# First transform with 64 points and two products a bank, U of the first block through scratch: an FNet and H3 kernel on one core of Trainium2

## The chip, the cores and the metric

The kernel runs on one core of one Trainium2 chip. The metric is the device time of one execution in microseconds (us). TensorE (PE) multiplies matrices, with its weight loads listed as PEld; VectorE (DVE), ScalarE (ACT) and GpSimd (POOL) work element by element; SyncE (SP) issues most transfers, ScalarE and GpSimd the others. All engines run their own lists of instructions in order and wait for each other by semaphores.

## The reference

x has 2048 rows (S) of 576 (D). Four layers are applied, A, B, A, B:

```python
x = x + _A_ref(layernorm(x), dft_seq_re, dft_seq_im, dft_hid_re, dft_hid_im)
x = x + _B_ref(layernorm(x), k, v, shift_k, ssm_k, ssm_D)
# and the same two once more

# A: a = x @ hid_re.T, b = x @ hid_im.T;  y = seq_re @ a - seq_im @ b
# B: k_shift = causal convolution of k with 4 taps;  kv = k_shift * v
#    y = irfft(rfft(kv, 4096) * rfft(ssm_k, 4096))[:2048] + kv * ssm_D;  y = q * y   (q is layernorm(x))
```

In B the part before the product with q depends on the inputs k, v, shift_k, ssm_k and ssm_D alone. It is the same for both B layers and is computed once.

## The kernel before

All large products are made on fp32 split into a rounded high part and a remainder (`split`: ScalarE writes the high part, VectorE the remainder), so that a product of two such numbers takes three TensorE instructions: high by high, high by low, low by high.

**The first A layer** runs over 128 steps (tb, g, k): four blocks of 512 output rows, two halves (real and imaginary DFT matrix, `c_mat`) and 16 pieces of the sum over the sequence. A step loads one 128 x 512 piece of c two steps ahead, splits it, and issues 14 products of 512 columns into four banks (s0 to s3) and one for the remaining 64 columns (rm). After 16 steps `evac_u` and `evac_r` split the banks into the chunks of U, nine of 128 x 1024 words in one region (`um`), which the next block overwrites. The rows X[j] of the normalized x are made in the first 16 steps (`get_x0`, `normed`, `to_x`).

**The hidden products** (`hidden`) multiply a finished block's U by W, the hidden DFT matrix: eight pieces a block, each 27 products of 288 columns into a bank (bk). They wait in `pending` and are issued by `finish` between the steps: odd steps of the next block, and what is left ahead of the last step of a half (`yield n, None`), because that step overwrites U. W is loaded and split by `load_w` from step `W_FROM` on, in the region where the branch kept k and its convolution, and is saved to scratch from step `W_SAVE` on.

**The branch** (`branch`) computes the part of B that depends on inputs alone, as a fast Fourier transform in stages, interleaved with the layer's steps. The first transform stage (`f1_split`, `f1_products`) has 32 items: 16 rows j from two sources, ssm_k and k_shift * v. For an item it multiplies by a 128-point matrix `fc`: two halves of 288 columns and two outputs, real and imaginary, three products a bank. ScalarE copies the bank out (`so`) and stores it to scratch (t). The convolution of k runs beside it on VectorE (`convolve`). From step `MID_FROM` on the middle stage loads t back: 64 mid groups of nine products and 32 inverse groups of six, spread by a count of work done (`spent`, `passed`, `total`) until step `I2_END`.

Where in the steps the first transform stands is set by these lines: up to step 16 `F1_16` sets the pace, then it is even until `F1_END` (42).

```python
at16 = 4 + 2 * F1_16
want = int(4 + F1_16 * at / 8 if at <= 16 else at16 + (68 - at16) * (at - 16) / (F1_END - 16))
```

**The second A layer** runs its first block in 32 such steps and the three others by Strassen's scheme; its 32 hidden pieces end the kernel. The last block's pieces of the first layer are issued between its first steps. The change does not touch it otherwise.

The order in which an engine's instructions stand is set by the program's order, by `behind` and `issue_after`, and by the framework's scheduling. Transfers through SP's queue are issued in order, one behind the other.

## Time and profile before

| | |
|---|---|
| median of 3 runs | 1202.72 us (1202.7 to 1205.96) |
| the profiled execution | 1201.11 us, span 1199.3 us |
| first product, last product of TensorE | 6.56 us, about 1191.6 us |
| busy: PE, DVE, ACT, POOL | 98%, 70%, 56%, 6% of the span |
| granted TensorE clock | 0.998 |
| moved by DMA | 261.96 MB, mean 218 GB/s |
| read from and written to HBM | 194.09 MB, 66.65 MB |

The page gives busy times for the whole span, 40 slices of it, groups of instructions and the chain of work that ended last. Its groups go by line, operation and tiles: bk<-f1r are the products of the first transform, bk<-mid those of the middle stage, bk<-w,u the hidden products of the first A layer, s and rm those of the steps. A group's mean is the length of one instruction; TensorE's instructions overlap, so their spacing is read from the timeline.

### The profile page before, as it was taken

What the parts mean: (1) busy time and instruction counts of PE and PEld (TensorE: products, weight loads), DVE (VectorE), ACT (ScalarE), POOL (GpSimd) and SP (SyncE); (2) the same over time, 40 slices, a digit from 0 to 9 for tenths busy, and PEclk for the clock granted to TensorE, in tenths of its full rate; (3) what the DMA queues carried; (4) which work ended last, traced back from release to release, by engine and by line L of the source; (5) the groups of instructions that cost most, each with busy time, mean ns of one, the idle gap of its engine ahead of it and who ended that gap; (6) DMA issues with size and microseconds to landing.
All of it is one profiled execution on the core that took longest, in us unless ns stands there. A gap on an engine that the chain in (4) does not pass through costs nothing.

```text
span 1199.3 us, 18263 instructions
## 1 busy us (share of the span) xinstructions
PE 1180.6 (98%) x6320; PEld 1026.0 (86%) x6320; DVE 839.9 (70%) x1498; ACT 665.9 (56%) x1335; POOL 75.5 (6%) x116
## 2 busy tenths in 40 slices
PE   7999999999999999999999999999999999999997
PEld 6888888988888888888988898888888888789997
DVE  7899883679777677675447766875676777774674
ACT  8855665679877768675435666544444435450210
POOL 2210000000000000001101121000000000001111
PEclk9999999999999999999999999999999999999999
DMA  9879898546656766658967686872772677794621
GB/s 340 308 226 318 275 304 256 177 133 182 216 177 199 213 180 207 187 149 249 305 202 236 222 257 213 271 264 71 216 281 74 207 275 269 237 347 142 214 96 40
DMA packets 146111, 261.96 MB, mean 218 GB/s; under 512 B 15841, under 2 KB 44769, under 8 KB 146018
## 3 DMA queue, kind: packets, MB, share of 16 engines
q1 hardware_dynamic: 102674, 205.58, 53.6%
q10 hardware_dynamic: 36432, 42.63, 10.3%
q0 software_dynamic: 6912, 12.59, 4.1%
q8 instruction: 49, 0.80, 0.3%
q14 instruction: 44, 0.36, 0.1%
HBM read 194.09 MB, written 66.65 MB: 217 GB/s over the span
## 4 chain that ended last, share of the span: by engine, by line
PE 84%; DVE 6%; DMA 4%; ACT 3%; issue 2%; POOL 1%; SPq 0%; POOLq 0%; DVEq 0%; ACTq 0%
PE s L74 46%; PE bk L74 33%; PE rm L74 5%; DMA flts<-in_c_mat 2%; ACT flts L486 1%; DVE mats L92 1%; DVE f1f L382 1%; DMA flts<-t 1%; POOL flts L616 1%; DVE mats L189 1%; ACT mid L486 1%; DVE f1f L387 0%; DMA t<-flts 0%; DVE u L92 0%; ACT mats L91 0%
## 5 line engine op out<-in xcount | busy, mean ns | idle before, releaser
L74 PE MATMUL s<-mats 128*128 128x512 f32 x2088 | 531.2, 392 | 0.8 <-DVE flts L613 0.3
L74 PEld LDWEIGHTS s<-mats 128*128 128x128 f32 x2088 | 381.1, 188 | 71.1 <-DVE mats L189 1.1
L92 DVE TENSOR_TENSOR mats<-flts,mats 128x512 fp32r<-128x512 f32 x206 | 140.7, 688 | 58.4 <-ACT mats L91 55.7
L91 ACT ACTIVATE mats<-flts 128x512 fp32r<-128x512 f32 x206 | 128.2, 627 | 85.4 <-PE bk L74 30.9
L74 PE MATMUL bk<-mid 128*128 128x288 f32 x768 | 131.1, 300 | 1.8 <-ACT flts L486 0.8
L74 PEld LDWEIGHTS bk<-mid 128*128 128x128 f32 x768 | 114.3, 188 | 21.2 <-ACT flts L486 8.4
L492 DVE TENSOR_TENSOR mid<-flts,mid 128x576 fp32r<-128x576 f32 (+1 forms) x160 | 101.9, 637 | 34.4 <-ACT mid L486 31.3
L74 PE MATMUL bk<-w,u 128*128 128x288 f32 x864 | 121.0, 296 | 0.7 <-DVE w L232 0.5
L74 PEld LDWEIGHTS bk<-w,u 128*128 128x128 f32 x864 | 117.4, 188 | 4.4 <-ACT flts L486 1.1
L486 ACT ACTIVATE flts<-bk 128x288 f32<-128x288 f32 x160 | 61.9, 404 | 87.4 <-PE bk L74 74.0
L74 PE MATMUL rm<-mats 128*128 128x512 f32 x304 | 94.9, 391 | 0.0
L486 ACT ACTIVATE mid<-flts 128x576 fp32r<-128x576 f32 (+1 forms) x159 | 86.8, 582 | 7.5 <-DMA flts<-t 3.7
L486 ACT ACTIVATE flts<-flts 64x288 f32<-64x288 f32 x192 | 85.0, 443 | 5.7
L432 ACT ACTIVATE flts<-bk 128x288 f32<-128x288 f32 x128 | 49.4, 408 | 47.0 <-PE bk L74 46.4
L74 PEld LDWEIGHTS bk<-f1r 128*128 128x128 f32 x384 | 59.5, 191 | 13.8 <-ACT f1r L91 7.4
L74 PE MATMUL bk<-f1r 128*128 128x288 f32 x384 | 64.5, 300 | 6.7 <-ACT f1r L91 6.7
L74 PE MATMUL bk<-mats 128*128 128x288 f32 (+1 forms) x376 | 67.8, 317 | 0.0
L74 PEld LDWEIGHTS rm<-mats 128*128 128x128 f32 x304 | 57.0, 188 | 12.1 <-DVE flts L264 0.3
L74 PE MATMUL s<-t,mats 128*128 128x512 f32 x264 | 64.9, 389 | 0.0
L278 DVE TENSOR_TENSOR flts<-flts,bk 128x288 f32<-128x288 f32 x48 | 21.7, 453 | 61.1 <-PE bk L74 58.8
L175 POOL TENSOR_TENSOR flts<-flts 128x1 f32<-128x1 f32 x35 | 28.9, 827 | 524.2 <-DVE flts L174 524.2
L74 PE MATMUL bk<-mats,t 128*128 128x288 f32 (+1 forms) x368 | 59.3, 303 | 0.0
(143 smaller groups left out, 1491.8 us busy)
## 6 DMA issues: line engine op xcount, KB each, us to landing
flts<-in_c_mat SPq DMA_DIRECT2D x148, 256.0 KB, 3.6
ph<-in_c_mat SPq DMA_DIRECT2D x54, 512.0 KB, 3.9
t<-flts ACTq DMA_DIRECT2D x64, 288.0 KB, 4.6
flts<-t SPq DMA_DIRECT2D x64, 288.0 KB, 2.9
flts<-in_c_mat SPq DMA_DIRECT2D x30, 512.0 KB, 5.3
vd<-flts ACTq DMA_DIRECT2D x64, 144.0 KB, 2.5
flts<-vd SPq DMA_DIRECT2D x32, 288.0 KB, 4.8
mid<-in_i2c POOLq DMA_DIRECT2D x32, 256.0 KB, 5.6
```

The costliest lines, as they stand in the source:

```text
L74: nc.tensor.matmul(ps, lhsT, rhs, start=first, stop=last, skip_group_check=more)
L91: a = nc.scalar.activation(h, src, AF.Copy).ins
L92: return a, nc.vector.tensor_tensor(l, src, h.bitcast(F32), OP.subtract).ins
L175: pows.append(nc.gpsimd.tensor_tensor(rs, ve, mhalf, OP.pow).ins)
L189: made.append(nc.vector.tensor_tensor(t[:, D + REM:], y[:, :NC * P], h[:, :NC * P], OP.subtract).ins)
L278: added[:] = [nc.vector.tensor_tensor(r[:, cs], r[:, cs], ps[:, :HD], OP.add).ins]
L382: nc.vector.tensor_tensor(out_t[:, n], k, wt[3 - t][:, n], OP.mult)
L432: stored[:] = [nc.scalar.activation(so[:, c, :], ps[:, :HD], AF.Copy).ins]
L486: last_act.append(nc.scalar.activation(*args, **kw).ins)
L492: nc.vector.tensor_tensor(l, src, h.bitcast(F32), OP.subtract)
L616: pows.append(nc.gpsimd.tensor_tensor(rs, sv, mhalf, OP.pow).ins)
```

## The change

The first transform has 64 points: on the host the rows of k, v and ssm_k are put in another order, even rows on partitions 0 to 63 and odd rows on 64 to 127, and the matrices are made for 32 sets of 64 rows. The split now puts the high part of 64 rows and their remainder on top of each other on 128 partitions, so that one product takes both; a bank needs two products, one with the high and one with the low part of the matrix. The stage's pace is `F1_PACE`, which ends at step 55.5. So W, which takes the convolution's place, is loaded from step 55 on. The first block's U is stored to scratch (`us_d`) chunk by chunk from step 33 on, loaded back in steps 72 to 76, and multiplied by W in steps 78 and 79; the second block's pieces come before, from step 64 on. The middle stage begins at step 61, and W is saved from step 80 on, every third step. The number and size of the transfers of t stay; the matrix of the middle stage now has 32 points on its first side.

```diff
-F1_END = 42
-W_FROM = 41
+F1_PACE = (0, 14, 16, 30, 32.5, 46, 48, 55.5), (4, 8.5, 9, 27, 28, 49.5, 50.5, 68)
+F1_END = 56
+W_FROM = 55
-W_SAVE = 60
-MID_LOAD = 44
-MID_FROM = 47
+W_SAVE = 80
+MID_LOAD = 57
+MID_FROM = 61
+SPILL = {33: 8, 36: 0, 39: 1, 42: 2, 45: 3, 51: 4, 54: 5, 57: 6, 60: 7}
+REFILL = {72: (0, 1), 73: (2, 3), 74: (4, 5), 75: (6, 7), 76: (8,)}
+PIECES = (*range(64, 72), 78, *range(97, 111, 2))
@@
-    t_d = [dr.tile([P, J, 2, 2, HD], F32, name=f"t{h}") for h in range(2)]
+    t_d = [dr.tile([P, 2, J, 2, HD], F32, name=f"t{h}") for h in range(2)]
+    us_d = [dr.tile([P, WIDE], F32, name=f"us{ch}") for ch in range(9)]
@@
+    spilled = []
+
+    def spill(ch):
+        load_after(us_d[ch], um[0][:, ch * WIDE:(ch + 1) * WIDE].bitcast(F32))
+
+    def refill(ch):
+        load_after(um[0][:, ch * WIDE:(ch + 1) * WIDE].bitcast(F32), us_d[ch])
+        if ch == 8:
+            pending.extend(spilled)
@@ layer
-                    pending.extend([us, tb, jj, xres, done] for jj in range(TB))
+                    (pending if tb else spilled).extend([us, tb, jj, xres, done] for jj in range(TB))
@@ f1_split
-            parted[:] = split(xf[0], xf[1], r)
+            sides = (xf[0], lo, hi), (xf[1], hi, lo)
+            if (j, src) == todo[0]:
+                h = [nc.scalar.activation(xf[0][lo], r[lo], AF.Copy).ins, nc.vector.tensor_copy(xf[1][hi], r[hi]).ins]
+            else:
+                h = [nc.scalar.activation(t[at], r[at], AF.Copy).ins for t, at, to in sides]
+            with behind(h[1]):
+                parted[:] = h + [nc.vector.tensor_tensor(t[to], r[at], t[at].bitcast(F32), OP.subtract).ins
+                                 for t, at, to in sides]
@@ f1_products
-                for c in range(2):
+                for h in range(2):
                     ps = bank()
-                    mm(ps[:, :HD], fc[:, c, :], xf[0][:, cs], True, False)
-                    mm(ps[:, :HD], fc[:, c, :], xf[1][:, cs], False, False)
-                    mm(ps[:, :HD], fc[:, 2 + c, :], xf[0][:, cs], False, True)
-                    stored[:] = [nc.scalar.activation(so[:, c, :], ps[:, :HD], AF.Copy).ins]
-                nc.scalar.dma_start(t_d[hf][:, j, :, src, :], so)
+                    mm(ps[:, :HD], fc[:, 2 * h, :], xf[h][:, cs], True, False)
+                    mm(ps[:, :HD], fc[:, 2 * h + 1, :], xf[h][:, cs], False, True)
+                    stored[:] = [nc.scalar.activation(so[:, h, :], ps[:, :HD], AF.Copy).ins]
+                nc.scalar.dma_start(t_d[hf][:, :, j, src, :], so)
@@ branch, its loop over the items
+            if n == 1:
+                yield from f1_products(*split_up.pop())
+                split_up.append((j, src, f1_split(j, src), fcs[j]))
+                f1_loads(n + 3)
+                continue
@@ the loop over the steps
-    first_lo = parted[1]
+    first_lo = parted[2]
     next(br)
     next(br)
     with behind(first_lo):
         get_x0(1)
-    next(br)
-    next(br)
+    with behind(*rounded):
+        next(br)
+        next(br)
...
-            at = n if whole else n - 0.5
-            at16 = 4 + 2 * F1_16
-            want = int(4 + F1_16 * at / 8 if at <= 16 else at16 + (68 - at16) * (at - 16) / (F1_END - 16))
+            want = int(np.interp(n if whole else n - 0.5, *F1_PACE))
...
-            if whole is None or whole and n % 2 == 1 and n % (2 * J) < J - 1 and pending:
+            if whole is None or whole and n in PIECES:
                 finish(pending, 1)
...
-        if n >= W_SAVE and n % 2 == 0:
+        if n in SPILL:
+            spill(SPILL[n])
+        for ch in REFILL.get(n, ()):
+            refill(ch)
+        if n >= W_SAVE and n % 3 == 0:
             next(wl, 0)
```

The changes of the host code (the order of the rows and the matrices) are left out.

More of the change, by code (lines that the diff above doesn't have):

```diff
@@ L338, in branch @@
     def branch():
+        lo, hi = slice(0, 64), slice(64, 128)
         f1r = region_b(FR, "f1r")
@@ L362, in load_k @@
                                   bass.AP(tensor=k_pad.tensor, offset=k_pad.offset + 2 * i * D,
-                                          ap=[[J * D, P], [1, 2 * D]]))
+                                          ap=[[(J + 4) * D, P], [1, 2 * D]]))
                 k_loaded[0] += 1
@@ L471, in branch @@
         load_fr(mc, midc)
-        lo, hi = slice(0, 64), slice(64, 128)
         def mid_half(df, o):
@@ L552, in load_feed @@
                 load_after(landed[i], v_d[hf][:, q].rearrange("p c d -> p (c d)") if kind else
-                           t_d[hf][4 * q:4 * q + 4].rearrange("q j c s d -> (q j c) (s d)"))
+                           t_d[hf][4 * q:4 * q + 4].rearrange("x h j s d -> (x h j) (s d)"))
         def load_fc(k):
@@ L1049, in _constants @@
     ang = 2 * np.pi * n / 8192
-    f1 = [_parts(np.cos(ang)), _parts(-np.sin(ang))]
-    f1c = np.stack([f1[0][0], f1[1][0], f1[0][1], f1[1][1]], axis=2)
-    at = ang.transpose(0, 2, 1)
+    h = P // 2
+    n = (32 * p[None, :h, None] + np.arange(2 * J)[:, None, None]) * (4 * q[None, None, :h] + 1) % 8192
+    f1 = np.stack([np.cos(2 * np.pi * n / 8192), -np.sin(2 * np.pi * n / 8192)], axis=3)
+    f1 = np.stack(_parts(f1.reshape(2, J, h, P)), axis=1).transpose(2, 3, 0, 1, 4).reshape(J, h, 4, P)
+    f1c = np.concatenate([f1, f1], axis=1)
+    at = ang.transpose(0, 2, 1)[:, (p % 2) * h + p // 2]
     i2 = [_parts(np.cos(at) / S), _parts(-np.sin(at) / S)]
@@ L1055, in _constants @@
     th = 2 * np.pi * (j[:, None] * r[None, :] % J) / J
-    f2 = np.zeros((4, J, 2, 2, 4, J))
     i1 = np.zeros((2, 4, J, 4, J, 2))
@@ L1059, in _constants @@
     for a in range(4):
-        f2[a, :, 0, 0, a, :] = c
-        f2[a, :, 1, 0, a, :] = s
-        f2[a, :, 0, 1, a, :] = -s
-        f2[a, :, 1, 1, a, :] = c
         i1[0, a, :, a, :, 0] = c.T
@@ L1067, in _constants @@
         i1[1, a, :, a, :, 1] = c.T
+    r = np.arange(2 * J)
+    th = 2 * np.pi * (r[:, None] * (r // J + r % J * 2)[None, :] % 32) / 32
+    f2 = np.zeros((2, 2, 2 * J, 2, 2, 2 * J))
+    c, s = np.cos(th), np.sin(th)
+    for a in range(2):
+        f2[a, 0, :, 0, a, :] = c
+        f2[a, 1, :, 0, a, :] = s
+        f2[a, 0, :, 1, a, :] = -s
+        f2[a, 1, :, 1, a, :] = c
     m = [*_parts(f2.reshape(P, P)), *_parts(i1.reshape(P, P))]
@@ L1080, in perm, with halved @@
         return m.transpose(1, 4, 3, 2, 0)
+    def halved(m):
+        return m.reshape(P // 2, 2, -1).transpose(1, 0, 2).reshape(P, -1, D)
     f1c, i2c, midc = _constants()
+    k = np.pad(a["B_k"][0], ((3, 1), (0, 0)))
     arrays = {
@@ L1087 @@
         "w_im": a["A_dft_hid_im"].T,
-        "k_pad": np.pad(a["B_k"][0], ((3, 1), (0, 0))),
-        "v": a["B_v"].reshape(P, J, D),
+        "k_pad": halved(np.stack([k[J * i:J * i + J + 4] for i in range(P)])),
+        "v": halved(a["B_v"]),
         "shift_k": a["B_shift_k"].T,
-        "ssm_k": a["B_ssm_k"].T.reshape(P, J, D),
+        "ssm_k": halved(a["B_ssm_k"].T),
         "ssm_d": a["B_ssm_D"],
```

## The prediction

> **What bounds the kernel now.** The first view is the page's table of busy times, with the rows of the 40 slices for TensorE (PE) and the DMA engines.
>
> ```profile
> PE 1180.6 (98%) x6320; PEld 1026.0 (86%) x6320; DVE 839.9 (70%) x1498; ACT 665.9 (56%) x1335; POOL 75.5 (6%) x116
> PE   7999999999999999999999999999999999999997
> DMA  9879898546656766658967686872772677794621
> ```
>
> TensorE is busy from the second slice to the last but one. Its busy time overlaps from product to product, so I take spacings instead, from the timeline (start, length, engine, what): one layer step without other work, the end of the kernel, and six first-transform products from the chain of waits.
>
> ```profile
> 628.50 2.88 PE L74 MATMUL s<-mats 128*128 128x512 f32 x12
> 631.68 2.88 PE L74 MATMUL s<-mats 128*128 128x512 f32 x12
> ```
> ```profile
> 1167.52 2.56 PE L74 MATMUL bk<-mats 128*128 128x288 f32 x18
> 1171.11 2.53 PE L74 MATMUL bk<-mats 128*128 128x288 f32 x18
> ```
> ```profile
> 194.18 0.79 PE bk L74 x6
> 194.97 1.37 PE s L74 x6
> ```
>
> A step (14 products of 512 columns) starts every 3.18 us, 0.227 each. Two bank fills (27 products of 288 columns) take 3.59 us, 0.133 each; six among layer products take 0.79, 0.132 each. I use 3.17 for a step (0.2266 a product) and 0.132. By its loops the kernel has 3,440 products of 512 columns and 2,880 of 288, together the page's 6,320: 779.5 + 380.2 = 1159.7 us of a span of 1199.3. Some 40 us are lost; the windows (PE, PEld, DVE, ACT, POOL busy, clock, DMA share, GB/s) show where.
>
> ```profile
> 0.00:20.78 20.78, 14.22 (x60) 11.61 (x61) 15.27 (x48) 15.67 (x26) 5.02 (x13) 1.00 0.97 335
> 20.78:70.26 49.48, 49.04 (x235) 40.78 (x234) 42.98 (x92) 41.55 (x89) 12.85 (x13) 1.00 0.86 297
> 70.26:200.17 129.91, 129.72 (x695) 112.52 (x694) 107.44 (x128) 77.08 (x172) 5.28 (x10) 1.00 0.88 278
> 200.17:618.72 418.55, 415.75 (x2371) 363.93 (x2370) 283.39 (x539) 286.12 (x615) 17.44 (x33) 1.00 0.65 200
> 618.72:1199.30 580.58, 571.83 (x2970) 497.22 (x2968) 390.86 (x693) 245.50 (x436) 34.87 (x48) 1.00 0.63 207
> 107.12:131.22 24.10, 24.10 (x133) 21.10 (x132) 24.06 (x27) 13.56 (x30) 1.58 (x3) 1.00 1.03 340
> 281.54:325.87 44.33, 44.33 (x235) 38.33 (x234) 37.26 (x75) 38.91 (x84) 0.00 (x0) 1.00 0.63 196
> ```
>
> The first five end at the start of steps 3, 16, 43 and 111 and at the end. The order of the program gives the products in each: 3 steps and 19 first-transform products, 12.0 of 20.78 us, 8.8 lost; 13 steps and 50, 47.8 of 49.48, 1.7 lost; 27 steps and 315, 127.2 of 129.91, 2.7 lost; 68 steps and 1,416, 402.5 of 418.55, 16 lost; the rest 11. So a product taken away is worth its spacing, unless another engine becomes late. VectorE (DVE) is the nearest: in 107.12 to 131.22 it is busy 24.06 of 24.10 us, and TensorE loses nothing.
>
> **The change part by part.**
>
> **1. Products, −16.9 us.** A bank of the first transform takes two products in place of three: 32 items with 4 banks each, 256 in place of 384. All have 128 rows, 128 columns and 288 moving columns as before, since the rounded part and the remainder of 64 rows are stacked into 128. 128 x 0.132 = 16.9. The Trainium skill, TensorE: Matmul & The Clock Gate, Back-to-back issue gap, gives N/2.4 + 2.5 ns, which is 122.5 ns for 288 columns and would make the saving 15.7 us; the trace's 0.132 decides.
>
> **2. Splits of the items.** One instruction over 128 partitions becomes two over 64, on ScalarE (ACT) and VectorE. Rows by form:
>
> ```profile
> L506 DVE TENSOR_TENSOR flts<-bk,flts 64x288 f32<-64x288 f32 x64 | 29.4, 459 | 1.7
> L505 DVE TENSOR_TENSOR flts<-bk,flts 128x288 f32<-128x288 f32 x64 | 29.1, 455 | 37.4 <-ACT flts L486 37.0
> L92 DVE TENSOR_TENSOR f1r<-f1f,f1r 128x576 fp32r<-128x576 f32 x16 | 12.0, 752 | 2.8 <-ACT f1r L91 2.7
> L91 ACT ACTIVATE f1r<-flts 128x576 fp32r<-128x576 f32 x16 | 10.9, 680 | 1.0 <-DMA flts<-in_ssm_k 1.0
> ```
>
> Half the partitions cost the same time, so VectorE gets 33 x 0.752 = 25 us more (65 in place of 32 instructions) and ScalarE 31 x 0.680 = 21 us (63 in place of 32). They hide under the layer's products as long as these engines have room. ScalarE has (77.08 of 129.91). For VectorE I take the back-to-back spacing.
>
> ```profile
> 120.00 1.35 DVE L382 TENSOR_TENSOR f1f<-f1f 128x1152 f32<-128x1152 f32 x1
> 121.27 0.75 DVE L92 TENSOR_TENSOR f1r<-f1f,f1r 128x576 fp32r<-128x576 f32 x1
> 121.94 1.35 DVE L382 TENSOR_TENSOR f1f<-f1f 128x1152 f32<-128x1152 f32 x1
> 123.21 0.68 DVE L92 TENSOR_TENSOR mats<-flts,mats 128x512 fp32r<-128x512 f32 x1
> 123.81 1.35 DVE L387 TENSOR_TENSOR f1f<-f1f 128x1152 f32<-128x1152 f32 x1
> ```
>
> 1.27 us for 1,152 elements, 0.67 for 576, 0.60 for 512. Between the c splits of steps 18 and 45 the changed order has on VectorE 38 convolution instructions of 1,152, 34 remainders of 576, 15 others of 576, and 39 of 512 columns: 48.3 + 22.8 + 10.1 + 23.4 = 104.6 us. TensorE has in the same 27 steps 85.6 + 126 x 0.132 = 102.2 us (before: 105.4 against 127.2). VectorE is thus at 102% over this stretch. What hides the excess is a lead: c splits run two to three steps (6 to 9 us) ahead, and the steps before are light on VectorE. Bounds: a gain of the 2.7 lost there now, and, if VectorE does only the 95% that would be 104.6/0.95 = 110, 8 us more. I take +2, near what the row with 24.06 of 24.10 shows can be had.
>
> **3. The start.** Fewer products of the branch lie in the first steps (8 in place of 19 before step 3), and VectorE's order changes. Rows of before:
>
> ```profile
> 8.96 0.68 DVE L189 TENSOR_TENSOR mats<-early,mats 128x512 fp32r<-128x512 f32 x1
> 9.56 0.68 DVE L92 TENSOR_TENSOR mats<-flts,mats 128x512 fp32r<-128x512 f32 x1
> 11.43 0.21 DVE L181 TENSOR_SCALAR flts<-flts 128x1 f32<-128x1 f32 x1 [0.32 <-POOL flts L175]
> 12.36 0.80 DVE L172 BATCH_NORM_STATS2 flts<-early 128x6 f32<-128x288 f32 x2
> 14.56 0.68 DVE L189 TENSOR_TENSOR mats<-early,mats 128x512 fp32r<-128x512 f32 x1
> 15.29 1.23 PEld L74 LDWEIGHTS s<-mats 128*128 128x128 f32 x6 [0.31 <-DVE mats L189]
> 17.52 0.68 DVE L189 TENSOR_TENSOR mats<-early,mats 128x512 fp32r<-128x512 f32 x1
> ```
>
> X[0] is complete at 9.64 and X[1] at 15.24, where step 1's products wait for it. In the changed order ten statistics (0.40 each) stand between the two, five before, and two c splits (0.60), one before; with eleven small ones (0.1) and X[1]'s own two (0.82) that is 4.0 + 1.2 + 1.1 + 0.8 = 7.1, plus about three waits of 0.3 for GpSimd's power: X[1] at 17.6. The first c remainder moves behind X[0], so step 0's second product starts at 10.3 and the step ends at 13.3. Then TensorE waits. Step 1 ends near 20.0; X[2] follows X[1] by four statistics and a c split, 3.8 us, at 21.4; step 2 ends near 23.4. From there X[3] and the later ones are ahead. Step 3 starts at 23.4 with 3 steps and 8 products done, 10.6 us: 12.8 lost in place of 8.8. **+4.0**, between +2 (the 2.4 of X[1] alone) and +5.
>
> **4. U of the first block through scratch.** Nine stores of 512 KB and nine loads, 9.44 MB, on SP's queue. A store is queued among the c loads, the operand loads and, from step 57 on, W's loads and the first t loads of the mid stage; the refills stand ahead of the c loads of steps 77 to 79. Who would wait: the split of U into chunks 0 to 3 at step 47 and 4 to 7 at step 63 (which holds the four s banks), and step 78, whose first hidden piece needs all nine refilled chunks. Rows for the room:
>
> ```profile
> DMA packets 8671, 13.27 MB, mean 332 GB/s; under 512 B 711, under 2 KB 5294, under 8 KB 8669
> flts<-in_c_mat SPq DMA_DIRECT2D x10, 256.0 KB, 4.5
> ```
>
> These are 95 to 135 us: 332 GB/s over 40 us and c landing in 4.5 us, in a stretch where TensorE lost nearly nothing. In the changed order steps 40 to 59 move 14.6 MB on SP's queue, 9.4 on ACT's and 2.1 on GpSimd's, 26.1 MB in 79.2 us of TensorE: 330 GB/s. Steps 72 to 78 have 37.6 us; at the mid stage's 200 GB/s that is 7.5 MB, and with 4.7 of refill 325 GB/s. Both are at what the trace has carried, none above it. Bounds 0 and 28.4 us (9.44 MB at 332 GB/s, none of it hidden). I take +2, near the lossless row. The Trainium skill, HBM Reference, Specifications, gives about 425 GB/s for a core that streams alone; by it the 26.1 MB need 61 of the 79.2 us and this term is 0. No row here holds such a rate over tens of microseconds.
>
> **5. Mid stage and W, 0 (−3 to +4).** 64 mid groups and 32 inverse groups go into steps 61 to 111 in place of 47 to 111, 12 products a step in place of 9. The c split on ScalarE:
>
> ```profile
> L91 ACT ACTIVATE mats<-flts 128x512 fp32r<-128x512 f32 x206 | 128.2, 627 | 85.4 <-PE bk L74 30.9
> ```
>
> In 281.54:325.87, ten steps with a group each, ScalarE is busy 38.91 of 44.33; with 0.63 a step for that split a group is 3.26, and 4/3 of it make 4.98 in a step of 3.17 + 12 x 0.132 = 4.75. Back-to-back instructions overlap (0.08 in the VectorE rows above), about eight a step, so it fits barely; over it would be 0.23 x 6 = 1.4 for steps 72 to 77. Against this the stage, which loses 16 now, is 14 steps shorter. The hand-over keeps its distance:
>
> ```profile
> 200.26 5.67 DMA t<-flts
> 208.06 5.81 DMA flts<-t
> 217.51 0.80 PE bk L74 x4
> ```
>
> A store of the last t (5.67), a load of t behind it (5.81) and two splits (0.68 + 0.75) make 12.9 us; the changed order has the layer products of steps 58 to 60 and six of step 61 there, 9.5 + 1.4 and two of the first transform, 11.2 us. Up to 1.7 us may show; such waits at the hand-over are in the 16 now. W's loads move with it (step 55, used at 63) and hide under steps 58 to 62, its saves move to steps 81 and later, and the number of hidden pieces stays.
>
> **Sum.** −16.9 + 2 + 4 + 2 + 0 = −8.9 against the profiled execution: 1201.11 us, 1192.2. The median of the runs, 1202.72, is 1.6 above it; less 8.9, **1193.8 us**. The terms' ends give 1188 to 1199. A difference under 0.3% (3.6 us) can't be told from no change.
>
> **The rivals.**
>
> **VectorE takes back the gain.** It can't run at 102% and does 95%: +8 in place of +2, 1199.8, and with one more microsecond at the mid stage no change. For: 71 to 100% busy already, two engines in turn on every item. Against: the row without loss.
>
> **All of it is kept.** The start costs 2, the others nothing: −15, 1187.7. For: the shorter mid stage; against: X[1]'s place in VectorE's order.
>
> **The scratch traffic holds TensorE: slower.** Place: steps 45 to 63 and 75 to 79. SP's queue is in order, so a spill or refill that lands late delays c loads, W and t loads together. Price: up to 28.4 us in place of 2. It decides from 14.5 us exposed (8.9 + 2 + 3.6), half of all; halfway between that and all, 21.5, the time is 1213. For: the DMA share is 0.88 over the whole stage and 1.03 at times, and c's landing is slow there. Against: the share of 0.65 at the refill, and that lossless stretch. By the skill's 425 GB/s it would not come to this.
>
> **How the numbers follow.** Forecast 0.58; all kept 0.12; VectorE 0.13; scratch traffic 0.17. Faster 0.70, same 0.13, slower 0.17. The range 1184 to 1206 takes in the first three with the unknown bounds (all kept and 3 us of the mid stage) and leaves out most of the last.
>
> **What would show it.** In the profile of the changed kernel: 256 bk<-f1r products at the same spacing; step 1 waiting for VectorE's L193 until about 17.6; steps 16 to 43 in 102 to 107 us with VectorE over 95% busy; the last bk<-f1r near 238; DMA share about 1 in steps 40 to 59; step 78 not waiting for u<-us; steps from 111 on as before. A stall of over 5 us ended by u<-us or in_c_mat, or steps 16 to 43 over 112 us, would make the prediction wrong, as would X[1] complete before 15.5.

## The result: 7 us slower, and the profile after

The changed kernel takes 1210.05 us in the median of 4 runs (1209.82 to 1212.36), the kernel before in runs beside it 1202.93 us. The ratio is 1.0058 with a 95% interval of 1.0037 to 1.0078: slower by more than the 0.3% that can be told apart, where 1193.8 us and "faster" were predicted. The profiled execution took 1212.36 us with a span of 1210.6, 11.3 us over the 1199.3 of before. It is the slowest of the four runs, 2.3 us over their median, and that of before was 1.8 under its own, so the profiles differ by 4 us more than the medians.

The first row is TensorE's of the busy table after. Below it are the windows that end at the start of steps 3, 16, 43, 59 and 111 and at the end (columns as before: busy time of PE, PEld, DVE, ACT, POOL, the clock, DMA share, GB/s).

```profile
PE 1175.5 (97%) x6192; PEld 1011.4 (84%) x6192; DVE 870.4 (72%) x1531; ACT 684.6 (57%) x1366; POOL 71.2 (6%) x116
```
```profile
0.00:22.61 22.61, 14.64 (x49) 10.89 (x50) 16.28 (x57) 15.13 (x25) 5.93 (x13) 1.00 0.85 292
22.61:69.76 47.15, 45.02 (x206) 37.09 (x204) 35.11 (x78) 41.30 (x84) 7.01 (x11) 1.00 0.81 269
69.76:179.99 110.23, 107.02 (x503) 87.97 (x504) 107.62 (x125) 66.81 (x135) 4.77 (x9) 0.98 0.84 259
179.99:245.66 65.67, 65.35 (x328) 55.24 (x326) 49.15 (x64) 45.78 (x97) 2.65 (x5) 1.00 0.83 271
245.66:629.68 384.02, 370.98 (x2143) 323.29 (x2144) 271.29 (x520) 269.69 (x590) 15.90 (x30) 1.00 0.71 223
629.68:1210.60 580.92, 572.46 (x2970) 496.91 (x2968) 390.94 (x693) 245.86 (x437) 34.93 (x48) 1.00 0.63 207
```

There are 128 products fewer (6192 for 6320), and steps 16 to 43 are 20 us shorter, mainly because they hold 126 products of the first transform in place of 315. But VectorE is busy 107.62 of the 110.23 us there, and the stretch from 245.66 to 629.68, the hand-over and the mid stage, takes 384 us for 52 steps and 1,416 products of 288 columns, 351.7 us by their spacings.

As in the prediction I count as lost what a stretch takes beyond 0.2266 us for a product of 512 columns and 0.132 for one of 288. Steps 16 to 43 after: 110.23 less 378 x 0.2266 and 126 x 0.132 is 7.9. The table has it in us for all kernels on which a conclusion rests, with the median of the runs and the ratio to the kernel before on the same chip. Beside the runs the kernel before took 1201.5 to 1203.3 us, so a difference between two medians of the table is known to about 2 us.

| kernel | steps 0-3 | 3-16 | 16-43 | 43-59 | 59-64 | 64-111 | median | ratio, 95% interval |
|---|---|---|---|---|---|---|---|---|
| before | 8.8 | 1.6 | 2.7 | 5.5 | 0.1 | 10.2 | 1202.9 | 1 |
| changed | 12.0 | 3.0 | 7.9 | 1.7 | 8.2 | 24.0 | 1210.05 | 1.0058 [1.0037, 1.0078] |
| schedule_only | 9.1 | 0.9 | 1.0 | 0.7 | 2.8 | 23.5 | 1212.36 | 1.0078 [1.0064, 1.0093] |
| stage_only | 12.6 | 10.9 | 24.9 | 13.7 | 0.1 | 9.8 | 1226.26 | 1.0202 [1.0188, 1.0216] |
| scratch_off | 12.5 | 3.0 | 6.8 | 1.1 | 6.7 | 22.7 | 1208.25 | 1.0050 [1.0038, 1.0063] |
| mid_from_52 | 9.4 | 1.3 | 3.5 | 2.0 | 1.0 | 16.0 | 1205.45 | 1.0027 [1.0016, 1.0038] |
| conv_less | 11.9 | 0.2 | 1.7 | 3.0 | 7.7 | 22.6 | 1201.31 | 0.9994 [0.9984, 1.0005] |
| mid_no_copies | 12.4 | 3.0 | 7.9 | 1.7 | 8.4 | 13.7 | 1199.43 | 0.9979 [0.9965, 0.9993] |
| before_no_copies | 10.0 | 1.0 | 2.9 | 5.4 | 0.1 | 6.2 | 1197.36 | 0.9958 [0.9943, 0.9973] |
| changed_relieved | 12.8 | 0.2 | 1.7 | 4.8 | 5.8 | 15.7 | 1194.31 | 0.9926 [0.9911, 0.9940] |
| before_relieved | 9.5 | 0.3 | 2.2 | 5.5 | 0.1 | 6.1 | 1195.25 | 0.9935 [0.9920, 0.9950] |
| mid_from_64 | 12.7 | 3.9 | 6.3 | 3.0 | 0.2 | 32.3 | 1212.81 | 1.0089 [1.0056, 1.0123] |

From before to changed the lost time grows by 3.2 + 1.4 + 5.2 − 3.8 + 8.1 + 13.8 and 0.3 behind step 111, 28.2 us; the products save 16.9; that is the 11.3.

The waits of TensorE's weight loads tell of the mid stage (columns: who waits for whom, us in total, times, longest). First 245.66 to 629.68 of the changed kernel, then 200.17 to 618.72 of before.

```profile
PEld bk L78 <- ACT flts L512: 18.1, 38, 1.4
PEld bk L78 <- DVE mid L518: 4.4, 14, 0.6
```
```profile
PEld bk L74 <- ACT flts L486: 9.5, 27, 0.8
PEld bk L74 <- DVE flts L507: 3.0, 7, 0.8
```

`flts` by L512 (before L486) is the copy of a product's bank by ScalarE. With three banks, TensorE can't begin a group's next fill until ScalarE has come round to that copy, and these waits now sum to twice what they did before.

### The profile page after: what moved, and what is told of

The parts are those of the page before. It is cut to its first block, busy times and chain, and to the rows that moved or that the text cites. A ratio compares the mean times of both kernels' runs of the same rounds, so it can differ in the third digit from the quotient of the medians.

```text
span 1210.6 us, 18119 instructions
## 1 busy us (share of the span) xinstructions
PE 1175.5 (97%) x6192; PEld 1011.4 (84%) x6192; DVE 870.4 (72%) x1531; ACT 684.6 (57%) x1366; POOL 71.2 (6%) x116
## 3 DMA queue, kind: packets, MB, share of 16 engines
q10 hardware_dynamic: 36432, 42.63, 10.2%
## 4 chain that ended last, share of the span: by engine, by line
PE 73%; DVE 9%; ACT 7%; DMA 6%; issue 4%; SPq 0%; POOL 0%; ACTq 0%; POOLq 0%; DVEq 0%
PE s L78 41%; PE bk L78 29%; PE rm L78 4%; ACT flts L512 3%; DVE f1f L398 2%; DMA flts<-in_c_mat 1%; DMA t<-flts 1%; DVE f1f L403 1%; DMA flts<-t 1%; DVE mats L96 1%; ACT mats L95 1%; ACT mid L512 1%; DVE f1r L442 1%; DVE mid L518 1%; DVE u L96 1%
## 5 line engine op out<-in xcount | busy, mean ns | idle before, releaser
L78 PE MATMUL s<-mats 128*128 128x512 f32 x2088 | 537.7, 394 | 6.5 <-DVE u L96 2.7
L78 PEld LDWEIGHTS s<-mats 128*128 128x128 f32 x2088 | 385.2, 189 | 82.4 <-DVE u L96 3.6
L78 PE MATMUL bk<-mid 128*128 128x288 f32 x768 | 134.8, 304 | 11.0 <-ACT flts L512 4.9
L78 PEld LDWEIGHTS bk<-mid 128*128 128x128 f32 x768 | 113.4, 188 | 34.0 <-ACT flts L512 15.8
L512 ACT ACTIVATE flts<-bk 128x288 f32<-128x288 f32 x160 | 61.2, 403 | 73.3 <-PE bk L78 59.1
L512 ACT ACTIVATE mid<-flts 128x576 fp32r<-128x576 f32 (+1 forms) x159 | 87.1, 582 | 17.0 <-DMA flts<-t 10.8
L512 ACT ACTIVATE flts<-flts 64x288 f32<-64x288 f32 x192 | 85.0, 443 | 6.2 <-ACT flts L512 0.2
L454 ACT ACTIVATE flts<-bk 128x288 f32<-128x288 f32 x128 | 46.7, 408 | 38.1 <-PE bk L78 33.2
L78 PEld LDWEIGHTS rm<-mats 128*128 128x128 f32 x304 | 57.2, 189 | 12.6 <-PE s L78 0.9
L78 PEld LDWEIGHTS bk<-mats 128*128 128x128 f32 x376 | 55.6, 188 | 3.4
L78 PEld LDWEIGHTS s<-t,mats 128*128 128x128 f32 x264 | 49.5, 188 | 10.4 <-DVE t L96 0.2
```

Of the source, the lines that this page charges most:

```text
L78: nc.tensor.matmul(ps, lhsT, rhs, start=first, stop=last, skip_group_check=more)
L454: stored[:] = [nc.scalar.activation(so[:, h, :], ps[:, :HD], AF.Copy).ins]
L512: last_act.append(nc.scalar.activation(*args, **kw).ins)
```

## The experiments

**Stage and schedule apart.** The change is two things, the stage with two products a bank and a schedule that stretches it. Each alone:

```diff
 stage_only: the changed kernel with
-F1_END = 56; W_FROM = 55; MID_FROM = 61; F1_PACE, SPILL, REFILL, PIECES
+F1_END = 42; W_FROM = 41; MID_FROM = 47; the pace of the kernel before
 schedule_only: the kernel before with
-F1_END = 42; W_FROM = 41; MID_FROM = 47
+F1_END = 56; W_FROM = 55; MID_FROM = 61; F1_PACE, SPILL, REFILL, PIECES
```

> The stage with 64 points and two products per bank in the schedule of the kernel before: first transform until step 42, W from 41, mid stage from 47, no scratch. VectorE has some 20 us more to do in steps 16 to 43, where it was busy 107.4 of 129.9 us, and TensorE 14 less: 127 of VectorE against 116 of TensorE. If VectorE takes the gain there, steps 16 to 43 take 126 to 131 us and the time is 1199 to 1204, even with the kernel before. If it does not (a lead or other order hides it), they take 116 to 120 and the time is 1188 to 1193. Steps 43 to 111 lose 14 to 18 us by either.

> The kernel before with the three products per bank, in the schedule of the change: first transform until step 55, scratch for the first block's U, mid stage from 61. 128 products (16.9 us) more than the changed kernel, and no further remainders on VectorE. If the loss is the schedule's, steps 59 to 111 lose 28 to 34 us as in the changed kernel and the time is 1216 to 1222. If the loss comes of the new stage (its stores, its remainders), they lose 14 to 20 and the time is 1202 to 1207.

Both are slower, 1226.26 and 1212.36. The stage alone is far over what its expectation gave. Windows of steps 16 to 43 of the one and the other:

```profile
80.27:216.70 136.43, 122.03 (x573) 97.46 (x574) 127.17 (x150) 88.72 (x185) 5.28 (x10) 0.96 0.81 252
```
```profile
66.28:178.23 111.95, 111.95 (x573) 96.37 (x572) 98.32 (x113) 56.05 (x117) 4.75 (x9) 1.00 0.82 261
```

The 127.17 us of VectorE are what was expected, but the stretch takes 136.43. VectorE is not the only one to hold it. Over steps 3 to 47 of stage_only the longest sum of waits of the weight loads is for ScalarE's copies of the first transform's banks, and these copies wait for a store of t to leave their buffer (0.3 us in the kernel before); the waits for VectorE's remainders of c and U come to 13.7.

```profile
PEld bk L77 <- ACT flts L453: 13.6, 12, 4.1
```
```profile
ACT flts L453 <- DMA t<-flts: 16.1, 13, 5.5
```

No run parts the two. The granted clock of 0.96 accounts for 5.1 of the 24.9 us lost. Steps 43 to 47 lose 7.7 (1.2 before): there TensorE waits for W, whose loads stand behind the late remainders. The schedule alone loses 1.0 us in steps 16 to 43, with VectorE at 98.32 of 111.95, and 26.3 in steps 59 to 111: the mid stage's loss is there without the new stage. It came out 4 us under its expectation, as steps 0 to 59 lose less than before. Read as a square, the schedule costs 9.4 us, and inside it the stage, whose products are worth 16.9, brings 2.3, which is within the scatter of the two.

**The scratch traffic.**

```diff
 the changed kernel with
-load_after(us_d[ch], um[0][:, ...])      # spill
-load_after(um[0][:, ...], us_d[ch])      # refill
```

> The changed kernel without the nine stores and nine loads of the first block's U; its eight hidden products read the second block's U again, so those rows of the output are another product of the same size. Everything else stays in place. If the scratch traffic holds TensorE, 8 to 18 us come back and the time is 1192 to 1202. If the loss of steps 59 to 111 (32.3 us) is that of the mid stage and its hand-over, 0 to 3 us come back: 1207 to 1210, with over 28 us still lost in steps 59 to 111.

1208.25, 1.8 us less, which is no difference beyond the scatter (ratio 1.0050, interval 1.0038 to 1.0063, against 1.0058 and 1.0037 to 1.0078): the rival that the traffic holds TensorE falls, and steps 59 to 111 still lose 29.4.

**A shorter mid stage without the rest.**

```diff
 the kernel before with
-MID_FROM = 47
+MID_FROM = 52     # hidden products still from 47
```

> The kernel before, its mid stage started at step 52 in place of 47; the first block's hidden products stay at step 47. So 59 steps and 16 hidden pieces (some 244 us of TensorE) cover the same 64 + 32 groups, as long as the 50 steps and 24 pieces of the changed kernel, but without scratch traffic and with the last t stored long before. If the density of the mid stage is what costs the 18 us more in the changed kernel, steps 43 to 111 lose 24 to 30 us in place of 16 and the time is 1211 to 1217. If the hand-over (the late last t, the queue on SP) or the scratch traffic costs it, the loss stays at 14 to 18: 1201 to 1205.

1205.45, 2.4 us more, between the two expectations and close to the second. Steps 64 to 111 lose 16.0 in place of 10.2, but steps 43 to 59 lose 2.0 in place of 5.5, so steps 43 to 111 lose 19.0 in place of 15.8. A shorter stage does cost, but 2.4 of the 8 to 14 us that I had put on it at this length. This stage is as long in time of TensorE as that of schedule_only, which costs 9.4, so most of what the schedule costs is not the stage's length.

**VectorE.** One tap of the convolution less, so that VectorE gives up about what the change has added:

```diff
 the changed kernel with
-for t in range(4):
+for t in range(3):
```

> The changed kernel with the fourth tap of the short convolution left out: 16 VectorE instructions of 1.35 us less (21.7 us, about what the change adds to VectorE), some 13 of them in steps 16 to 43; everything else in place. If VectorE's load is what costs 7.9 us in steps 16 to 43, it is busy about 90 of 104 us there, the loss falls to 1 to 2 us and the time to 1202 to 1205. If the order or the waits between the half-height splits cost it, the loss stays over 5 and the time over 1207. Steps 59 to 111 keep 30 to 33 us by either.

1201.31, 8.7 us less. Steps 3 to 16 and 16 to 43:

```profile
22.45:66.79 44.34, 44.34 (x205) 37.04 (x204) 32.64 (x75) 40.81 (x83) 7.02 (x11) 1.00 0.83 279
66.79:170.77 103.98, 103.77 (x506) 87.58 (x505) 97.77 (x117) 67.10 (x136) 4.76 (x9) 1.00 0.86 279
```

VectorE is still busy 97.77 of 103.98, 94% (90 us were expected), and TensorE loses 1.7; at 107.62 of 110.23 it lost 7.9. That shows VectorE's load as the cause of what steps 3 to 43 lose, 9.0 of the 10.9. Where it is lost is shown by windows of the changed kernel, steps 16 to 33 and 33 to 43, and by the waits of the weight loads over both.

```profile
69.76:140.18 70.42, 67.21 (x306) 54.10 (x307) 69.28 (x83) 40.92 (x82) 3.18 (x6) 0.98 0.76 226
140.18:179.99 39.81, 39.81 (x199) 33.87 (x198) 38.34 (x43) 25.90 (x53) 1.59 (x3) 1.00 0.98 318
```
```profile
PEld s L78 <- DVE u L96: 3.1, 2, 2.2
PEld bk L78 <- DVE f1r L442: 3.1, 7, 1.0
PEld s L78 <- DVE mats L96: 1.4, 4, 0.5
```

Steps 16 to 33 lose 7.5 of the 7.9 us, with VectorE at 98%. They end with the split of U, whose four remainders join VectorE's queue at once, and after that wait the clock falls for 3.4 us, 1.7 of the 7.5. Behind them VectorE is 96% busy and TensorE is busy throughout.

**VectorE's work on GpSimd.** The same relief with nothing left out:

```diff
 rem_pool: the changed kernel, stage_only_rem_pool: stage_only, with
-nc.vector.tensor_tensor(t[to], r[at], t[at].bitcast(F32), OP.subtract)
+nc.gpsimd.tensor_tensor(...)             # items from j = 4 on
```

> The changed kernel with the two remainders of the items from j = 4 on (48 of 64 instructions) on GpSimd instead of VectorE. If VectorE is what costs 7.9 us in steps 16 to 43 (busy 107.6 of 110.2), it falls to some 82 us there, the loss to 1 to 3 us as in the schedule with three products, and the time to 1203 to 1206. If the order of the two half-height splits or GpSimd's own pace holds TensorE, the loss stays over 6 or grows and the time is 1209 or more. Steps 59 to 111 keep their 32 us by either.

> The stage of two products in the schedule of the kernel before (1226.3 us, VectorE busy 127.2 of 136.4 us in steps 16 to 43), with the remainders from j = 4 on on GpSimd. If VectorE is what makes it slow, it goes to about 95 us there, steps 3 to 43 lose 4 to 8 us in place of 35.8, and the time is 1192 to 1199, less than the kernel before. If GpSimd's remainders are too slow for an item every 4 us or the other part of the new stage (loads, stores) holds it, the time stays over 1210.

1237.38 and 1260.5, 27 and 34 us more. Rows by form of rem_pool, the first two of GpSimd, the rest of VectorE; then VectorE's rows of the changed kernel in steps 16 to 43:

```profile
L443 POOL TENSOR_TENSOR f1r<-flts,f1r 64x576 fp32r<-64x576 f32 x24 | 49.1, 2046 | 23.7 <-ACT f1r L440 20.8 <-issue 1.6
L443 POOL TENSOR_TENSOR f1r<-f1f,f1r 64x576 fp32r<-64x576 f32 x24 | 48.4, 2015 | 25.8 <-ACT f1r L440 24.6
```
```profile
L96 DVE TENSOR_TENSOR mats<-flts,mats 128x512 fp32r<-128x512 f32 x206 | 161.7, 792 | 66.0 <-ACT mats L95 61.6 <-PE bk L78 1.6 <-PE rm L78 1.5
...
L398 DVE TENSOR_TENSOR f1f<-f1f 128x1152 f32<-128x1152 f32 x28 | 43.4, 1555 | 4.6 <-POOL f1r L443 4.3
L403 DVE TENSOR_TENSOR f1f<-f1f 128x1152 f32<-128x1152 f32 x24 | 39.7, 1654 | 0.2
```
```profile
L398 DVE TENSOR_TENSOR f1f<-f1f 128x1152 f32<-128x1152 f32 x21 | 28.3, 1353 | 0.2
L403 DVE TENSOR_TENSOR f1f<-f1f 128x1152 f32<-128x1152 f32 x16 | 21.7, 1354 | 0.2
L96 DVE TENSOR_TENSOR mats<-flts,mats 128x512 fp32r<-128x512 f32 x27 | 18.5, 688 | 1.0 <-ACT mats L95 0.7
L442 DVE TENSOR_TENSOR f1r<-f1f,f1r 64x576 fp32r<-64x576 f32 x22 | 16.6, 754 | 0.7
```

GpSimd takes 2.03 us for what VectorE does in 0.754, and VectorE's own instructions grow, on the mean over the run, from 1353 to 1555, from 1354 to 1654 and from 688 to 792 ns. So nothing was relieved (VectorE is busy 115.54 us in steps 16 to 43, 107.62 without it), and the run says nothing on VectorE as the cause. The Trainium skill, SBUF — State Buffer, SBUF: two separate sides, says that a VectorE instruction with two SBUF inputs and a GpSimd one take one port pair in turn, each holding it to its end; the longer rows agree with that.

**ScalarE in the mid stage.** The three copies of a group, 85 us of ScalarE, on GpSimd and then left out:

```diff
 mid_copies_pool: act(kk[..], kk[..], AF.Copy) x3  ->  nc.gpsimd.tensor_copy / tensor_scalar
 mid_no_copies, before_no_copies:
-act(kk[lo, 1, :], kk[hi, 0, :], AF.Copy); act(kk[hi, 1, :], ..., scale=-1.0); act(kk[hi, 0, :], kk[lo, 0, :], ...)
+products with kk[hi, 0, :] and kk[lo, 0, :] in place
```

> The changed kernel with three of the mid group's copies (the two halves exchanged and the negated one, 64 rows each) on GpSimd instead of ScalarE. If ScalarE's load is behind the waits for banks in steps 61 to 111 (17.4 us in 37 waits for its copies out of the banks), the loss of 32 us falls by 8 to 16 and the time is 1194 to 1202. If the chain of a group's steps through three banks is the limit, the loss stays or grows with GpSimd's slower copies: 1209 to 1216.

> The changed kernel with the three 64-row copies of each mid group left out (192 x 0.443 = 85 us of ScalarE in steps 61 to 111), the products reading the uncopied halves, which is another product. If ScalarE's load or its place in the chain is behind the waits for banks, the loss of steps 64 to 111 falls from 24 to 8 to 14 us and the time to 1194 to 1201. If three banks and the order of products on TensorE are the limit, it stays at 20 or more and the time over 1206.

> The kernel before with the three 64-row copies of each mid group left out as in mid_no_copies (the products read the uncopied halves, another product). If the waits behind ScalarE's copies are there in the same number before and cost little because the stage is longer, the loss of steps 47 to 111 (14.5 us) falls by 2 to 5 and the time is 1198 to 1201: then most of what the copies cost in the changed kernel (10.6 us) is due to the shorter stage. If they cost as much per group in either schedule, 9 to 11 come back and the time is 1192 to 1194.

On GpSimd the time is 1222.57, 12.5 us more and over both expectations: the copies take longer (the negated one 1.09 us there, 0.44 on ScalarE), which fits a longer chain of a group but does not show it, as instructions of VectorE grew too (those of L534 from 452 to 525 ns).

```profile
L524 POOL TENSOR_SCALAR flts<-flts 64x288 f32<-64x288 f32 x64 | 69.9, 1092 | 4.3
```

Left out, 10.6 us come off the changed kernel and 5.0 off the kernel before, 0.6 more than expected. Steps 64 to 111 of the changed kernel with and without the copies, and the waits without them over 245.96 to 619.88:

```profile
274.58:629.68 355.10, 346.36 (x2040) 304.17 (x2039) 251.78 (x487) 250.47 (x553) 15.90 (x30) 1.00 0.70 220
```
```profile
273.38:619.88 346.50, 342.97 (x2052) 305.78 (x2052) 250.25 (x489) 171.31 (x372) 15.86 (x30) 1.00 0.72 226
```
```profile
PEld bk L78 <- ACT flts L512: 9.4, 27, 2.7
```

ScalarE was busy only 250 of 355 us, 71%, and taking a third of that away halved the waits for it, from 18.1 to 9.4 us. On the mean the engine was not full; it came late. The same copies cost 10.3 us of steps 64 to 111 in the changed kernel and 4.0 in the kernel before, so about 6 of the 13.8 are the copies in the new schedule.

Most of the 13.8 lies in steps 79 to 95: they lose 9.3 more than before, steps 64 to 79 lose 1.5 more and 95 to 111 lose 3.0 more. Of the 11.4 lost there now, 4.5 are lost in a single stretch behind the start of step 79, where the last seven pieces of the first block (189 products) stand with 84 products of mid groups. The kernel before has the like stretch behind step 47, among its first groups. Windows of the two, changed and before:

```profile
391.39:435.12 43.73, 42.02 (x289) 39.01 (x288) 31.31 (x65) 31.06 (x71) 0.53 (x1) 1.00 0.52 152
```
```profile
218.02:258.19 40.17, 39.97 (x282) 37.68 (x281) 29.17 (x61) 27.07 (x60) 0.00 (x0) 1.00 0.47 148
```

They lose 4.5 and 2.0 us by the spacings. schedule_only loses the same 4.5 there, mid_no_copies 1.4. In mid_from_52, which issues these pieces ahead of its stage, steps 79 to 95 lose 3.6, against 8.9 in schedule_only. That the place of the pieces makes this difference is likely but not shown: no run moves them alone.

**The hand-over at steps 59 to 64.**

```diff
 t_on_pool_queue:    load of t: nc.sync.dma_start  ->  nc.gpsimd.dma_start
 first_t_from_input: the first four groups' data from x[:, i, :] instead of t
 mid_from_64:        MID_FROM = 61 -> 64, MID_LOAD = 57 -> 60
```

> The changed kernel with the mid stage's loads of t issued on GpSimd's queue instead of SP's, so that no c, W or scratch transfer stands behind a t load that waits for a store. If SP's order is what makes steps 59 to 64 lose 8.2 us, 3 to 6 of them come back: 1204 to 1207. If the late last t itself is the cause, steps 59 to 64 lose 7 to 9 as now: 1209 to 1212.

> The changed kernel with the first four mid groups' data read from the input x instead of t, so that neither they nor the transfers behind them on SP's queue wait for the last stores of t; the four groups compute with other numbers. If that wait is the 8.2 us of steps 59 to 64, 5 to 7 come back: 1203 to 1206. If c, W and U's own work crowd ScalarE and VectorE there, 0 to 2 come back: 1208 to 1211.

> The changed kernel with its mid stage started at step 64 in place of 61 and its first loads issued at 60 in place of 57. If the hand-over (t's last store, W's splits and the first groups at once on ScalarE) costs the 8.2 us of steps 59 to 64, these fall to 1 to 3; the denser stage behind takes 2 to 6 of that back: 1206 to 1210. If the steps' own c splits and U's evacuation cost it, 6 or more stay there and the time is 1211 to 1215.

What the hand-over of the changed kernel waits for first is the chain of t. A store of t issued at 243.21 takes 6.68 us, the first load of t is issued when it has landed, at 249.96, and ScalarE waits for that load.

```profile
243.21 6.68 DMA t<-flts
```
```profile
253.75 0.68 ACT L514 ACTIVATE mid<-flts 128x576 fp32r<-128x576 f32 x1 [6.29 <-DMA flts<-t]
```

The second load of t stands behind three of W on SP's queue and lands at 257.8, a load of c behind it takes 6.68 us to 260.67, and steps 61, 62 and 63 lose 3.0, 3.6 and 1.5 us.

t's loads on GpSimd's queue cost 8.7 us more (1218.76). Steps 59 to 64 lose 7.8, so taking t out of SP's order doesn't help; steps 64 to 79 lose 2.8 more, and 5.7 are lost behind step 111, of which 2.2 are the granted clock and the rest is open. With the first groups' data from x, steps 59 to 64 lose 5.9 in place of 8.2, but the time is 1211.6: no gain that can be measured, and not a clean test, since the new loads land in buffers that the last stores of t still hold. In the third the loss moves. Windows of steps 59 to 64 and 64 to 111 of mid_from_64, and its waits over both:

```profile
246.87:262.88 16.01, 15.77 (x69) 13.06 (x70) 10.02 (x15) 8.93 (x16) 0.00 (x0) 1.00 1.03 349
262.88:631.27 368.39, 355.90 (x2075) 310.95 (x2074) 261.57 (x506) 262.08 (x575) 15.84 (x30) 0.99 0.70 217
```
```profile
PEld bk L78 <- ACT flts L512: 26.4, 50, 3.9
```

The hand-over's loss is gone, 0.2 us for 8.2, and as much is back behind: 32.3 us for 24.0, where 2 to 6 were expected. Three steps later means three steps fewer for the same groups, but steps 59 to 111 lose 32.5 in place of 32.2, no more than with three steps more. 2.2 of the 8.3 that came back are in the stretch behind step 79, and 3.2 in step 104 (5.4 lost, 2.1 in the changed kernel), where TensorE waits once for a load of the inverse groups' matrix:

```profile
578.20 0.37 PE L78 MATMUL bk<-mid 128*128 128x288 f32 x1 [3.53 <-DMA mid<-in_i2c]
```

So the run shows that the hand-over's wait goes when the loads of t come later, and that it brought nothing; that both losses are one sum, set by the number of steps, it does not show.

**W's stores.**

```diff
 the changed kernel with
-W_SAVE = 80 (every third step)
+W_SAVE = 111 (every step)
```

> The changed kernel with W's nine stores to scratch behind step 111 instead of between 81 and 105. If these stores make the mid stage's t loads late (up to 5.2 us near 450 us) and that costs the 11.4 us of steps 79 to 95, 3 to 6 come back: 1204 to 1207. If the mid stage's own chain costs it, 0 to 1.5 come back: 1208.5 to 1211.

1209.17, no difference beyond the scatter; steps 79 to 95 lose 9.1 in place of 11.4.

**Fewer stacked items, where VectorE has room.**

```diff
 the schedule of before, 64 points, and per item
+if item in TWO:   # stacked: two products of 128 rows, two remainders of 64
+else:             # one remainder of 128 rows, three products of 64 rows
```

> The schedule of the kernel before, without scratch, with the 64-point transform for all 32 items, but the stacked split with two products a bank only for 11 of them (the last eight, where VectorE has no convolution left, and three before); the other 21 keep one rounding and one remainder over 128 rows and take three products of 64 rows. 44 products fewer (5.8 us) and 11 remainders more on VectorE (8.3 us), the pace a little slower to step 36 and faster behind. If VectorE's room decides what a saved product is worth, 3 to 6 us come off the kernel before: 1197 to 1200. If products of 64 rows cost more than those of 128, or the stacked split costs TensorE wherever it stands, the time is 1203 or more.

> As mixed_11_items, but the stacked split for the last twelve items, which reach into steps where VectorE is full. If VectorE's room decides, the four items from 20 to 23 cost as much as they bring: 1198 to 1202, 0 to 2 us above mixed_11_items. If not, it is the faster of the two by 0.5.

1211.53 and 1213.26, 9 and 11 us over the kernel before: neither expectation's gain came. The products of 64 rows are one reason. From mixed_11_items, weight loads by form, and TensorE's timeline around one item:

```profile
L76 PEld LDWEIGHTS bk<-f1r 64*128 64x128 f32 x252 | 23.6, 191 | 25.2 <-issue 9.9 <-ACT f1r L93 6.4 <-ACT mats L93 2.5
...
L76 PEld LDWEIGHTS bk<-f1r 128*128 128x128 f32 x88 | 14.9, 188 | 2.4 <-DVE u L94 0.2
```
```profile
92.90 0.62 PE L76 MATMUL rm<-mats 128*128 128x512 f32 x2
93.45 0.67 PE L76 MATMUL bk<-f1r 64*128 64x288 f32 x6
94.06 1.66 PE L76 MATMUL s<-mats 128*128 128x512 f32 x6
```

Among themselves they start every 121 ns (median of 200), but each change between 64 and 128 rows costs: from one of them to a layer product 221 ns, where 133 stand between a product of 128 rows and a layer product, and into them 319 in place of 227. Some 0.18 us for each group of them, about 50 groups: 9 us, less 2 for their shorter spacing. The other is that remainders of the last items delay W (steps 43 to 59 lose 13.7). No version that beats the kernel before came of this.

**Both reliefs together.**

```diff
 changed_relieved, before_relieved: conv_less and mid_no_copies in one
```

> The changed kernel with both the fourth tap of the convolution and the three copies of each mid group left out. If the two are separate places of the loss, their gains add up (8.7 and 10.6): 1189 to 1193. If the time given back in one comes back as a loss in the other, 1195 to 1199.

> The kernel before with the same two parts left out. If VectorE had room before, the tap is worth 0 to 2 there and the copies 5.0 as in before_no_copies: 1195 to 1198, some 5 above the changed kernel with the same parts left out, so that the change pays where VectorE and ScalarE have room. If the changed kernel's loss is in something else, this one is the faster of the two: under 1190.

1194.31 and 1195.25: with room on VectorE and ScalarE the change, 7.1 us slower as it stands, comes out level with the kernel before (intervals of the ratios 0.9911 to 0.9940 and 0.9920 to 0.9950). Two expectations are missed. The gains in the changed kernel add up to 15.7, not 19.3, as steps 43 to 59 and 95 to 111 lose more; and the change doesn't come out 5 us ahead. Steps 59 to 111 lose 21.5 in the one and 6.2 in the other, even without the copies.

## Why the prediction was wrong

**Products, −16.9: right.** 128 fewer, and the median from one bk<-f1r to the next is still 132 ns. The formula that the prediction sets beside it is no rival: the Trainium skill, TensorE: Matmul & The Clock Gate, Back-to-back issue gap, calls it the gap of a single isolated product and not that of a stream with a weight load each.

**The start, +4.0: 3.2 measured.** The rows of X[1] and X[2] on VectorE, and of step 1, which waits for the first:

```profile
16.22 0.68 DVE L193 TENSOR_TENSOR mats<-early,mats 128x512 fp32r<-128x512 f32 x1
...
19.96 0.69 DVE L193 TENSOR_TENSOR mats<-early,mats 128x512 fp32r<-128x512 f32 x1
```
```profile
16.95 2.36 PE L78 MATMUL s<-mats 128*128 128x512 f32 x9 [0.24 <-DVE mats L193]
```

X[1] is complete at 16.9 (17.6 predicted), step 3 starts at 22.61 (23.4).

**Splits of the items, +2: mis-sized, 5.2 in steps 16 to 43 and 1.4 in steps 3 to 16.** The 104.6 us of VectorE against 102.2 of TensorE were counted rightly. What failed is "I take +2, near what the row with 24.06 of 24.10 shows can be had". That row holds for 24 us. In the 70 us of steps 16 to 33 the lead did not last, and the whole stretch took 110.2, the value worked out for 95%. The first rival was right in this place, though not by an engine that can do only 95%: behind step 33 VectorE is 96% busy and nothing is lost. The lead of the c splits was not what failed first, as only 1.4 us of waits are for c; the remainders of the items and of U came late, 3.1 us each. Relieving VectorE gave 9 us.

**U through scratch, +2: 1.8 by the medians** of scratch_off, within the scatter, so between nothing and the 2 that were taken. The rival of the scratch traffic has its sign and nearly its time (1213), but by luck and not by its mechanism: no long wait was ended by u<-us.

**Mid stage and W, 0 (−3 to +4): this is the step that failed.** Steps 43 to 111 lose 33.9 us in place of 15.8, +18.1, far outside its bounds. Two sentences failed. The first, that "the stage, which loses 16 now, is 14 steps shorter" was taken for a gain, as if the loss grew with the number of steps. The groups are the same, and their loss did not fall: in steps 59 to 111 it is 10.3 us before, 17.0 in mid_from_52, 26.3 in schedule_only and 32.2 after the change. The second, the reckoning by ScalarE's busy time, 4.98 us of work in a step of 4.75, was made for steps 72 to 77 alone. There it was not far off (1.4 expected, 2.6 lost, ScalarE 89% busy), but the other steps of the stage were put at nothing, and over steps 64 to 111, where ScalarE is 71% busy on the mean, the time goes in some 40 waits of half a microsecond for a bank.

Of the hand-over, which "keeps its distance", "up to 1.7 may show"; it was 8.1 more than before. The chain of the first load was sized about right: from the start of the store at 243.21 to the first group's second half at 255.28 it took 12.1 us (12.9 predicted), and TensorE waited 1.0 us for that group. What was left out is that the next loads, of t, W and c, stand in the same queue and land late too, and that the clock falls after these waits. About 6 us of the stage's part are shown to be ScalarE's copies. What makes the rest of the stage's part stays open: the stretch behind step 79 is where the largest piece of it lies, and scratch and W's stores by themselves showed no difference beyond the scatter.

**The sum.** One figure of it doesn't come out: the terms' ends, added up, give 1182 to 1205 us and not 1188 to 1199, with the scratch traffic at 2 or less, and more with its upper bound.

**What would show it** didn't show it: X[1] at 16.9, steps 16 to 43 under 112 us, no wait of TensorE over 5 us ended by u<-us or in_c_mat. None of the signs named for a wrong prediction came, and the result was still of the other sign, because none was named for the length of the steps from 61 to 111, which I had put at zero. Three of the signs named for a right one were missed: steps 16 to 43 took 110.2 us and not 102 to 107, the last bk<-f1r came at 242.3 (238 predicted), and the DMA share in steps 43 to 59 was 0.83, not about 1.

## What to carry to other kernels

A stage can lose time with no engine full on the mean: then the row to read is the wait for the buffer that turns over (three banks here), not the busy share, and a shorter stretch for the same groups is no gain until these waits are priced. Work that frees the first engine is worth its spacing only as long as what it loads on the second leaves the second some room: in steps 16 to 43 VectorE's work was 0.96 of TensorE's own time in conv_less, where 1.7 us were lost, 1.05 in the changed kernel with 7.9, and 1.14 in stage_only with 24.9, not all of it VectorE's. A row at 100% for 24 us is no proof for 110. Where a change joins a cheaper stage with a new schedule, price and run each alone: here the schedule cost 9.4 us by itself, more than the stage brought in it.

## What the hardware showed unexpectedly

After a string of short waits the granted clock falls here, and the wait is paid twice. At the hand-over of the changed kernel TensorE waits 1.59 us, and the next twelve layer products, 2.88 us elsewhere, take 4.09; the first window shows the granted clock of the step, the second that of the 3.4 us in which it is halved.

```profile
265.83 0.37 PE L78 MATMUL bk<-mid 128*128 128x288 f32 x1 [1.59 <-ACT mats L95]
...
267.69 4.09 PE L78 MATMUL s<-mats 128*128 128x512 f32 x12
```
```profile
267.45:274.58 7.13, 7.13 (x34) 6.02 (x34) 6.79 (x14) 6.88 (x15) 0.00 (x0) 0.81 0.56 157
266.80:270.21 3.41, 3.41 (x11) 2.87 (x11) 3.13 (x8) 3.32 (x8) 0.00 (x0) 0.50 0.60 185
```

Such a piece costs 1.7 us. Steps 16 to 43 hold one in the changed kernel and three pieces' length in stage_only (10.24 us); the kernel before has none ahead of step 111.

The Trainium skill, TensorE: Matmul & The Clock Gate, A second HAM failure mode: psum-queue depth-cycling, describes this: a TensorE that idles briefly and often between groups as it cycles through banks is throttled and warmed again, and throughput falls with it. The 0.50 for 3.4 us agrees. The other two are told above: in rem_pool GpSimd lengthens VectorE's instructions with two inputs by 15 to 22% on the mean, and a change between products of 64 and of 128 rows costs about 90 ns each way.
